# Window attention and a two-layer FFN on one core: in which order blocks and weight tiles are passed at the start

## The chip, the cores and the metric

The kernel runs on one core of a Trainium2 chip. The metric is the device time in microseconds. Three runs of the kernel before gave 1069.83, 1072.06 and 1072.11 us, so 1072.06 us is the median.

## The reference

Eight batches of 576 positions and eight heads of 64 go through causal attention with a window of 64 positions; the result, 4608 tokens by 512, goes through a matrix, a softplus and a second matrix.

```python
scores = scale * np.matmul(q, k.transpose(0, 1, 3, 2))
mask = (rel >= 0) & (rel < window)           # rel = query position - key position, window = 64
scores = np.where(mask, scores, -1000000000.0)
attn = np.exp(scores - np.max(scores, axis=-1, keepdims=True))
attn = attn / (np.sum(attn, axis=-1, keepdims=True) + 1e-09)
x = np.matmul(attn, v)                       # to 4608 x 512
h = x @ w_in                                 # 512 x 2048
g = np.maximum(h, 0.0) + np.log1p(np.exp(-np.abs(h)))
out = g @ w_out                              # 2048 x 512
```

All inputs and the output are float32 to the caller; the weights lie in DRAM as float64, and the kernel takes each weight apart into a high and a low part itself.

## The kernel before, in words

The 4608 tokens are cut into 12 blocks of 384 (`TB`). `g` numbers the blocks in the order in which they are worked on. For each block there is an attention part, made of four head pairs (`hp`, two heads each), and an FFN part, made of 16 steps, one for each tile of 128 hidden features (`f`, "weight tile" below). One step (`g`, `f`) is `ffn_up`, 12 matmuls of 384 columns into a bank `ps_h` (line 450; of `ps_h` there are two), a softplus on ScalarE and VectorE (lines 454 to 461; line 458 is the one that reads `ps_h` last), and `ffn_down`, 9 matmuls of 512 columns that add into three banks `ps_o` (line 471). The x of a block, which is what attention makes and `ffn_up` reads, stands in eight tiles, high and low for each head pair, and there are two such sets ("sides").

A weight tile has to be made before its first use: `load_w(f)` loads two pieces of float64, and each piece takes one instruction on ScalarE (161), four on VectorE (162 to 165; the first four pieces have line 162 on GpSimd), a rounding on ScalarE (166) and a subtraction on GpSimd (167). The two pieces come out as `osb` on VectorE. Weight tiles 8 to 15 stand in memory that the attention of blocks 0 and 1 uses before.

Attention of blocks 0 and 1 uses TensorE for its transposes (`by_pe`); from block 2 on q and k are transposed by DMA, whose input is `nat` and whose output is `tr` (line 314). In its stages a head pair runs scores (334), a masked minimum on VectorE (342), exp on ScalarE (345), sum, reciprocal and product (352, 353, 358), transposes back (379, 380), a split (385, 386), the product with v (427) and the x of this head pair (431, 432, 139, 140).

Since all weight tiles are not ready at the start, the FFN does not go through the blocks one by one. `passes` lists which block takes which range of tiles: block 0 over tiles 0 to 7, block 1 over all 16, block 0 over 8 to 15, and then block after block. A block whose range ends before tile 15 stores its partial sums to DRAM (`spill`), and they are added when the rest is done (`fill`). In this text step 0 to 191 are numbered in the order of `passes`.

What sets the order of the instructions is a list of events with due times: step n has its up part at 2n + 0.5 and its down part at 2n + 3.5; `load_w(f)` stands 12 before its first use; the head pairs of the first blocks begin at `BASE[g] + PACE[g] * hp`. The list is sorted and emitted. For events before 100 (steps up to 47) a scheduler then orders the instructions of every engine, so that an instruction can be put ahead of others that were emitted sooner; behind that TensorE keeps the emitted order. Each engine executes its own list strictly in that order on the chip.

Of the kernel before, what the change touches and what calls it, by code (L numbers as in the profile page):

```python
# [8 lines left out]
F32 = mybir.dt.float32  # L9
BF16 = mybir.dt.bfloat16  # L10
F32R = mybir.dt.float32r
# [4 lines left out]
P = 128  # L16
TB = 384
# [3 lines left out]

SPLIT = 8
AHEAD = 12
BASE = (-100, -46, 2 * (SPLIT + 16) - 24)
PACE = (5, 5, 4)
STG0 = (-8, 1, 3, 4, 5, 7, 8, 9, 10)
STG2 = (-8, 0, 2, 3, 4, 6, 7, 8, 9)
STG = (-13, -5, 0, 0, 3, 5, 7, 8, 11)
# [8 lines left out]
def window_attention_softplus_ffn(  # L37
# [16 lines left out]
    nc = tc.nc  # L54
    B, H, S, D = q.shape
    NT, DM = out.shape
    DF = w_in.shape[1]
    NP = H // 2
    NC = DM // P
    NF = DF // P  # L60
    NB = NT // TB
# [9 lines left out]
    xp = ctx.enter_context(tc.tile_pool(name="xp", bufs=1))  # L71
    ff = ctx.enter_context(tc.tile_pool(name="ff", bufs=2))
    late = ctx.enter_context(tc.tile_pool(name="late", bufs=1))
    dram = ctx.enter_context(tc.tile_pool(name="dram", bufs=1, space=bass.MemoryType.DRAM))
# [42 lines left out]
    def weight(m, i, f):  # L117

        if f < NE:
            return w_first[m][i][:, f, :]  # L120
        k = (f - NE) // 4
        if (m, i, k) not in w_last:
            w_last[m, i, k] = spare(4 * k + 2 * m + i, [P, 4, DM], F32R, f"w{m}{i}{k}")
        return w_last[m, i, k][:, f % 4, :]
# [19 lines left out]
    def raw_tiles(f):  # L144

        ks = (5,) if f < NE else [k for k in (5,) if k >= 4] if f < NE + 4 else []
        at = f % (len(ks) + 1)
        if at == len(ks):
            return [ff.tile([P, NC, P], w_in.dtype, name="raw", bufs=2) for _ in range(2)]
        t = spare(ks[at], [P, 2, NC, P], w_in.dtype, "raws")  # L150
        return [t[:, m, :, :] for m in range(2)]

    def float64_split(dst_hi, dst_lo, src, raw, n):


        nc.sync.dma_start(raw, src)
        words = raw.bitcast(U32).rearrange("p c (n two) -> p two c n", two=2)
        low, high = words[:, 0, :, :], words[:, 1, :, :]
        w = ff.tile([P, NC, P], F32, name="osb", bufs=2)
        wb = w.bitcast(U32)  # L160
        nc.scalar.activation(w, high.bitcast(F32), AF.Abs)
        (nc.gpsimd if n < 4 else nc.vector).tensor_scalar(w, w, ZERO_HIGH, None, ALU.max)  # L162
        nc.vector.tensor_scalar(wb, wb, 3, 0x3FFFFFF8, ALU.logical_shift_left, ALU.bitwise_and)  # L163
        nc.vector.scalar_tensor_tensor(wb, high, 0xC0000000, wb, ALU.bitwise_and, ALU.bitwise_or)  # L164
        nc.vector.scalar_tensor_tensor(wb, low, 29, wb, ALU.logical_shift_right, ALU.bitwise_or)  # L165
        nc.scalar.copy(dst_hi, w)
        nc.gpsimd.tensor_tensor(dst_lo, w, dst_hi.bitcast(F32), ALU.subtract)

    def load_w(f):
        fs = slice(f * P, (f + 1) * P)  # L170
        raws = raw_tiles(f)
        for m, src in enumerate((w_in[:, fs].rearrange("(c p) n -> p c n", p=P), w_out[fs, :].rearrange("p (c n) -> p c n", n=P))):
            hi, lo = [weight(m, i, f).rearrange("p (c n) -> p c n", n=P) for i in range(2)]
            float64_split(hi, lo, src, raws[m], 2 * f + m)
# [55 lines left out]
    xs = {}  # L230
    taken_ps = [0]

    def attention(g, hp):
# [39 lines left out]
        if by_pe:  # L273
# [17 lines left out]
            for hh in range(2):  # L291
                rows = slice(hh * D, (hh + 1) * D)
# [30 lines left out]
        for j in range(NJ):  # L323
            first = j == 0 and not prev
            c0 = WIN if first else 0
            n = W - c0
# [62 lines left out]

        if hp == 0:  # L390
            xs[g] = [[None] * NP, [None] * NP]
        side = 0 if g == 0 else 1 if g == 1 else (g + 1) % 2
        x_t = [xp.tile([P, TB], F32R, name=f"x{i}_{hp}_{side}") for i in range(2)]
        for i in range(2):
            xs[g][i][hp] = x_t[i]
        if by_pe:
# [3 lines left out]
        for hh in range(2):  # L400
# [6 lines left out]
            for kb in reversed(range(NJ)):  # L407
                n = W if kb < NJ - 1 else P
# [26 lines left out]
            yield  # L435


    gs = {}
    ops = {}
    part = {}  # L440
# [23 lines left out]
    def ffn_down(g, f, first, last):  # L464
        gt = gs.pop((g, f))
        if first:
            ops[g] = [ps_o.tile([P, DM], F32, name=f"ps_o{j}") for j in range(NJ)]
        for j in range(NJ):
            js = slice(j * P, (j + 1) * P)
            for i, (a, b) in enumerate(((0, 0), (0, 1), (1, 0))):  # L470
                mm(  # L471
                    ops[g][j], gt[a][:, js], weight(1, b, f),
                    start=(first and i == 0), stop=(last and i == 2),
                )
        if last:
            rows = out[ORDER[g] * TB : (ORDER[g] + 1) * TB, :]
            spill, fill = f < NF - 1, f == NF - 1 and g in part
            if spill:
                part[g] = rows = dram.tile([TB, DM], F32, name="part")
            for j0, j1 in ((0, 2), (2, 3)):  # L480
                o = ff.tile([P, NC, P], w_in.dtype, name="raw", bufs=2).bitcast(F32)
                o = o.rearrange("p c n -> p (c n)").rearrange("p (j n) -> p j n", n=DM)[:, : j1 - j0, :]
                rs = slice(j0 * P, j1 * P)
                if fill:
                    nc.sync.dma_start(o, part[g][rs, :].rearrange("(j p) n -> p j n", p=P))
                for j in range(j0, j1):
                    if fill:
                        nc.vector.tensor_tensor(o[:, j - j0, :], o[:, j - j0, :], ops[g][j], ALU.add)
                    else:
                        (nc.scalar.copy if j == 1 else nc.vector.tensor_copy)(o[:, j - j0, :], ops[g][j])  # L490
                nc.sync.dma_start(rows[rs, :].rearrange("(j p) n -> p j n", p=P), o)
# [2 lines left out]

    passes = [(0, 0, SPLIT), (1, 0, NF), (0, SPLIT, NF)] + [(g, 0, NF) for g in range(2, NB)]
    steps = [(g, f, f == f0, f == f1 - 1) for g, f0, f1 in passes for f in range(f0, f1)]


# [2 lines left out]
    events = []  # L503
    for g in range(NB):
        for hp in range(NP):
            if g < 3:
                base = BASE[g] + PACE[g] * hp
            else:
                base = 2 * NF * (g - 1) + SHP * hp + SH
            stages = attention(g, hp)  # L510
            for at in STG if g >= 3 else STG2 if g >= 2 else STG0:
                events.append((base + at, lambda stages=stages: next(stages, None)))
    loaded = 0
    for n, (g, f, first, last) in enumerate(steps):
        if f == loaded:
            events.append((2 * n - AHEAD, lambda f=f: load_w(f)))
            loaded += 1
        events.append((2 * n + 0.5, lambda g=g, f=f: ffn_up(g, f)))
        events.append((2 * n + 3.5, lambda step=steps[n]: ffn_down(*step)))
    events.sort(key=lambda e: e[0])  # L520
    for at, emit in events:
        if at < PE_ORDERED_FROM:
# [34 lines left out]
```

## Time and profile before

| | us |
|---|---|
| three runs, median (lowest, highest) | 1072.06 (1069.83, 1072.11) |
| the profiled execution's own time | 1069.74 |
| its span, first to last instruction | 1067.9 |
| TensorE (PE) busy | 1028.4, 96% of the span |
| VectorE (DVE) busy | 789.0, 74% |
| ScalarE (ACT) busy | 650.0, 61% |
| GpSimd (POOL) busy | 224.7, 21% |

The span is what the rows of the profile divide up; the profiled execution's own time is 1.84 us longer, and the median of the three runs lies 2.3 us above that. "Busy" adds up the time in which an engine had an instruction; a row of a group gives source line, engine, operation, output and input tiles, shape, count, busy time, mean duration in ns and the idle time ahead of it. Since instructions of an engine overlap a little, means times counts come out above the busy time.

### The profile page before, as it was taken

How to read it: one execution, taken by the hardware profiler on the slowest of the kernel's cores; microseconds unless marked ns; L12 is line 12 of the kernel's file. 1: busy time of each engine (PE TensorE's matmuls, PEld its weight loads, DVE VectorE, ACT ScalarE, POOL GpSimd, SP SyncE). 2: the span in 40 equal slices, each digit the busy share in tenths (PEclk: the TensorE clock that was granted, in tenths of full speed). 3: DMA queues.
4: the chain of work that ended last, by engine and by line, in shares of the span. 5: the costliest groups of instructions: out<-in, count | busy, mean ns of one | idle time of the engine just before them, and what ended most of it. 6: DMA issues, size and time to landing. Idle time of an engine off the chain costs nothing.

```text
span 1067.9 us, 18172 instructions
## 1 busy us (share of the span) xinstructions
PE 1028.4 (96%) x6096; PEld 924.3 (87%) x6096; DVE 789.0 (74%) x2319; ACT 650.0 (61%) x1669; POOL 224.7 (21%) x217
## 2 busy tenths in 40 slices
PE   7797988999999999999999999999999999999998
PEld 5576867888999899999999999999999999999996
DVE  4999899866777777777777777777777777865433
ACT  6786666666665666566656666656666665655333
POOL 4354355631111111112111111111211111110000
PEclk9999998999999999999999999999999999999999
DMA  7754645255334434343344334424434533520000
GB/s 197 198 140 105 169 105 146 67 127 119 70 71 101 96 79 105 64 97 81 81 96 96 84 76 93 107 60 88 102 74 84 115 80 62 131 51 1 30 1 30
DMA packets 296222, 98.20 MB, mean 92 GB/s; under 512 B 280512, under 2 KB 288704, under 8 KB 296128
## 3 DMA queue, kind: packets, MB, share of 16 engines
q1 hardware_dynamic: 296128, 97.03, 40.0%
q8 instruction: 48, 0.79, 0.3%
q14 instruction: 46, 0.38, 0.1%
HBM read 50.07 MB, written 10.22 MB: 56 GB/s over the span
## 4 chain that ended last, share of the span: by engine, by line
PE 78%; DVE 12%; DMA 4%; ACT 3%; issue 2%; SPq 1%; POOL 0%; DVEq 0%; ACTq 0%
PE ps_h L450 32%; PE ps_o L471 31%; PE ps_a L334 5%; PE ps_a L427 4%; PE ps_a L380 2%; DMA tr<-nat 2%; PE ps_a L379 2%; DVE p_t L358 2%; DVE osb L165 2%; DVE osb L164 1%; DVE osb L162 1%; DVE p_t L342 1%; DVE osb L163 1%; SPq L198 1%; DVE u L458 1%
## 5 line engine op out<-in xcount | busy, mean ns | idle before, releaser
L450 PE MATMUL ps_h<-x,w 128*128 128x384 f32 x2304 | 458.4, 344 | 15.4 <-DVE u L458 11.8
L471 PE MATMUL ps_o<-w,g 128*128 128x512 f32 x1728 | 438.7, 397 | 6.3 <-ACT g L460 4.3
L450 PEld LDWEIGHTS ps_h<-x,w 128*128 128x128 f32 x2304 | 400.6, 189 | 27.5 <-DVE u L458 12.5
L471 PEld LDWEIGHTS ps_o<-w,g 128*128 128x128 f32 x1728 | 318.1, 188 | 65.6 <-ACT g L460 4.6
L458 DVE SCALAR_TENSOR_TENSOR u<-ps_h,u 128x384 f32<-128x384 f32 x192 | 106.0, 552 | 139.7 <-ACT u L456 139.5
L454 ACT ACTIVATE u<-ps_h 128x384 f32<-128x384 f32 x192 | 93.6, 488 | 179.4 <-PE ps_h L450 177.2
L345 ACT ACTIVATE p_t<-p_t,mn 128x192 f32<-128x192 f32 (+1 forms) x288 | 127.0, 443 | 63.5 <-DVE mn L342 63.2
L140 POOL TENSOR_TENSOR x<-xf,x 128x384 fp32r<-128x384 f32 x40 | 41.1, 1027 | 460.6 <-DVE rs L352 362.9
L358 DVE TENSOR_SCALAR p_t<-p_t,rs 128x192 f32<-128x192 f32 (+1 forms) x288 | 110.4, 429 | 2.9
L342 DVE CUSTOM_DVE_ANT_0 p_t<-ps_a,mask 128x192 f32<-128x192 f32 (+1 forms) x244 | 77.3, 343 | 46.5 <-PE ps_a L334 36.1
L455 ACT ACTIVATE u<-u 128x384 f32<-128x384 f32 x192 | 100.7, 526 | 4.1
L456 ACT ACTIVATE u<-u 128x384 f32<-128x384 f32 x192 | 100.6, 524 | 3.2
L461 DVE TENSOR_TENSOR g<-u,g 128x384 fp32r<-128x384 f32 x160 | 89.5, 559 | 3.8 <-DVE g L460 0.5
L385 ACT CAST pt<-ps_a 128x512 fp32r<-128x512 f32 (+1 forms) x144 | 59.0, 417 | 33.7 <-PE ps_a L380 21.9
L312 POOL TENSOR_TENSOR nat<-q_in,nat 128x384 bf16<-128x384 f32 x40 | 38.6, 965 | 187.8 <-ACT nat L311 152.1
L386 DVE TENSOR_TENSOR pt<-ps_a,pt 128x512 fp32r<-128x512 f32 (+1 forms) x144 | 67.9, 477 | 12.3 <-ACT pt L385 10.7
L334 PE MATMUL ps_a<-tr 128*128 128x192 bf16 (+1 forms) x720 | 74.8, 246 | 0.9 <-DVE xf L432 0.7
L460 DVE CAST g<-u 128x384 fp32r<-128x384 f32 x176 | 67.9, 386 | 5.9
L380 PE MATMUL ps_a<-ident,p_t 128*128 128x128 f32 x276 | 66.6, 276 | 1.4 <-DVE p_t L358 1.3
L427 PEld LDWEIGHTS ps_a<-pt,vt 128*128 128x128 f32 (+1 forms) x608 | 64.0, 163 | 3.9 <-issue 0.5
L427 PE MATMUL ps_a<-pt,vt 128*128 128x64 f32 (+4 forms) x608 | 64.5, 247 | 0.4 <-DVE mn L342 0.4
L431 ACT COPY xf<-ps_a 64x384 f32<-64x384 f32 x80 | 38.1, 477 | 40.3 <-PE ps_a L427 37.5
(91 smaller groups left out, 1019.3 us busy)
## 6 DMA issues: line engine op xcount, KB each, us to landing
out_dram<-raw SPq DMA_DIRECT2D x12, 512.0 KB, 3.2
q_in<-in_q_dram SPq DMA_DIRECT2D x56, 96.0 KB, 2.6
raw<-in_moe_w_in_dram SPq DMA_DIRECT2D x10, 512.0 KB, 4.2
raw<-in_moe_w_out_dram SPq DMA_DIRECT2D x10, 512.0 KB, 4.2
k_in<-in_k_dram SPq DMA_DIRECT2D x32, 128.0 KB, 3.5
v_in<-in_v_dram SPq DMA_DIRECT2D x32, 128.0 KB, 2.8
raws<-in_moe_w_in_dram SPq DMA_DIRECT2D x6, 512.0 KB, 4.2
raws<-in_moe_w_out_dram SPq DMA_DIRECT2D x6, 512.0 KB, 5.0
```

What stands on the lines that cost most here:

```text
L334: mm(spv[:, hh, :], tr_q[a][:, hh, j * P : (j + 1) * P], tr_k[b][:, hh, kc], start=(hh == 0 and i == 0), stop=(hh == 1 and i == 2), skip_g ...
L342: nc.vector.tensor_tensor_reduce(pv, spv[:, hh, :], m[:, c0:], 1.0, 3.0e38, ALU.add, ALU.min, mn[:, j, hh : hh + 1])
L345: nc.scalar.activation(pv, pv, AF.Exp, bias=mn[:, j, hh : hh + 1], scale=-1.0, accum_out=sm[:, j, hh : hh + 1])
L358: nc.vector.tensor_scalar(pv, pv, rs[:, jj, hh : hh + 1], None, ALU.mult)
L427: mm(av[: D if lo else P, osl], vt[:, vb, hh, : 1 if lo else 2, :], pt[hh][lo][:, psl], start=(i == 0), stop=(i == len(order) - 1), skip_g ...
L450: mm(hv, weight(0, a, f)[:, c * P : (c + 1) * P], x[b][c], start=(i_mm == 0), stop=(i_mm == 3 * NC - 1))
L454: nc.scalar.activation(u, hv, AF.Abs)
L455: nc.scalar.activation(u, u, AF.Exp, scale=-1.0)
L456: nc.scalar.activation(u, u, AF.Ln, bias=1.0)
L458: nc.vector.scalar_tensor_tensor(gf, hv, 0.0, u, ALU.max, ALU.add)
L461: (nc.vector if g >= 2 else nc.gpsimd).tensor_tensor(gt[1], gf, gt[0].bitcast(F32), ALU.subtract)
L471: mm(ops[g][j], gt[a][:, js], weight(1, b, f), start=(first and i == 0), stop=(last and i == 2),)
```

## The change

The passes become: blocks 0 and 1 over tiles 0 to 7, block 2 over all 16, then block 1 over 8 to 15, then block 0 over 8 to 15, then block 3 and so on. With that:

- `BASE` and `PACE` get an entry for block 3, and block 2's attention is due from 8 on, where it was due from 24 on.
- `load_w` of tiles 8 to 15 is due at 10, 14.5, and so on to 41.5, where it was 12 ahead of its first use (20, 22, and so on to 34).
- The side of x is `g % 2`, so that block 2 takes the side of block 0, and block 3 that of block 1. Block 0's x is needed again later: `keep_x` stores its eight tiles (384 floats by 128 partitions each) to DRAM, and `fetch_x` loads them back after block 2's last step.
- Block 1 now has partial sums too; they get a DRAM tile of their own.

```diff
-BASE = (-100, -46, 2 * (SPLIT + 16) - 24)
-PACE = (5, 5, 4)
+LATE, LATE_PACE = 10, 4.5
+BASE = (-100, -46, 4 * SPLIT - 24, 69)
+PACE = (5, 5, 4, 5)
...
-        side = 0 if g == 0 else 1 if g == 1 else (g + 1) % 2
-        x_t = [xp.tile([P, TB], F32R, name=f"x{i}_{hp}_{side}") for i in range(2)]
+        x_t = [xp.tile([P, TB], F32R, name=f"x{i}_{hp}_{g % 2}") for i in range(2)]
...
+    x_kept = dram.tile([2 * NP, P, TB], F32, name="x_kept")
+
+    def keep_x():
+        for i in range(2):
+            for hp in range(NP):
+                nc.sync.dma_start(x_kept[i * NP + hp, :, :], xs[0][i][hp].bitcast(F32))
+
+    def fetch_x():
+        xs[0] = [[xp.tile([P, TB], F32R, name=f"x{i}_{hp}_0") for hp in range(NP)] for i in range(2)]
+        for i in range(2):
+            for hp in range(NP):
+                nc.sync.dma_start(xs[0][i][hp].bitcast(F32), x_kept[i * NP + hp, :, :])
...
-                part[g] = rows = dram.tile([TB, DM], F32, name="part")
+                part[g] = rows = dram.tile([TB, DM], F32, name=f"part{g}")
...
-    passes = [(0, 0, SPLIT), (1, 0, NF), (0, SPLIT, NF)] + [(g, 0, NF) for g in range(2, NB)]
+    passes = [(0, 0, SPLIT), (1, 0, SPLIT), (2, 0, NF), (1, SPLIT, NF), (0, SPLIT, NF)]
+    passes += [(g, 0, NF) for g in range(3, NB)]
...
-            if g < 3:
+            if g < len(BASE):
...
-            events.append((2 * n - AHEAD, lambda f=f: load_w(f)))
+            at = 2 * n - AHEAD if f < SPLIT else LATE + LATE_PACE * (f - SPLIT)
+            events.append((at, lambda f=f: load_w(f)))
...
+    events.append((SPLIT + 0.7, keep_x))
+    events.append((2 * (2 * SPLIT + NF) + 0.7, fetch_x))
```

How it moves the instructions is seen at three places. The lines of the changed kernel are one higher from line 27 on and 14 higher from the FFN on: its 163 to 166 are 162 to 165 of before, 343 is 342, 353 and 354 are 352 and 353, 359 is 358, 464 is 450, 472 is 458, 474 and 475 are 460 and 461, and 485 is 471.

First, VectorE around the line 458 of step 16 (the 17th step). Before, where step 16 is block 1 with tile 8, it is row 378 of VectorE's list:

```order
L432 TENSOR_TENSOR xf_1704<-ps_a_1787,xf_1704 64x384
L164 SCALAR_TENSOR_TENSOR osb_1548<-raw_1533,osb_1548 128x512
L386 TENSOR_TENSOR pt01_1811<-ps_a_1816,pt00_1810 128x64
L310 SCALAR_TENSOR_TENSOR q_in_1515<-q_in_1515,nat_1954 128x384
L313 COPY nat_1954<-nat_1954 128x6x64
L310 SCALAR_TENSOR_TENSOR k_in_1516<-k_in_1516,nat_1954 128x512
L313 COPY nat_1954<-nat_1954 128x8x64
L165 SCALAR_TENSOR_TENSOR osb_1548<-raw_1533,osb_1548 128x512
L458 SCALAR_TENSOR_TENSOR u_1778<-ps_h_1765,u_1778 128x384
L162 TENSOR_SCALAR osb_1627<-osb_1627 128x512
```

Now, where step 16 is block 2 with tile 0, it is row 508; the two rows with `raw_2238` belong to the last of the 32 weight pieces, and `rs_2751` and `pt01_2893` to the first head pair of block 3:

```order
L165 SCALAR_TENSOR_TENSOR osb_2249<-raw_2238,osb_2249 128x512
L353 TENSOR_SCALAR rs_2751<-sm_2750 128x2
L166 SCALAR_TENSOR_TENSOR osb_2249<-raw_2238,osb_2249 128x512
L387 TENSOR_TENSOR pt01_2893<-ps_a_2898,pt00_2892 128x64
L354 RECIPROCAL rs_2751<-rs_2751 128x2
L472 SCALAR_TENSOR_TENSOR u_2044<-ps_h_2031,u_2044 128x384
L359 TENSOR_SCALAR p_t00_101<-p_t00_101,rs_2751 128x192
L359 TENSOR_SCALAR p_t01_102<-p_t01_102,rs_2751 128x192
L472 SCALAR_TENSOR_TENSOR u_2103<-ps_h_2090,u_2103 128x384
L474 CAST g0_2049<-u_2044 128x384
```

What moved: 130 more rows stand ahead of step 16's line 458, among them the last six weight pieces and most of block 3's first head pair.

Second, TensorE at the up part of step 18. Before, its bank is `ps_h_1967`, its x that of block 1, and the transposes behind it are of block 2's attention:

```order
L450 MATMUL ps_h_1967<-x0_3_1_700,w000_1217 128x384
L450 MATMUL ps_h_1967<-x1_3_1_701,w000_1217 128x384
L450 MATMUL ps_h_1967<-x0_3_1_700,w010_1218 128x384
L380 MATMUL ps_a_1889<-ident_85,p_t11_104 128x128
L379 MATMUL ps_a_1889<-ident_85,p_t11_104 128x128
```

Now its bank is `ps_h_2124`, its x that of block 2, and the transposes behind it are of block 3's attention; `ps_h_2175` is step 19, and `g0_2049` with `ps_o0_2112` and its neighbours is the down part of step 16:

```order
L464 MATMUL ps_h_2124<-x0_3_0_1918,w00_109 128x384
L464 MATMUL ps_h_2124<-x1_3_0_1919,w00_109 128x384
L464 MATMUL ps_h_2124<-x0_3_0_1918,w01_110 128x384
L380 MATMUL ps_a_2899<-ident_85,p_t00_101 128x128
L381 MATMUL ps_a_2899<-ident_85,p_t00_101 128x128
L464 MATMUL ps_h_2175<-x0_0_0_1369,w00_109 128x384
L464 MATMUL ps_h_2175<-x1_0_0_1370,w00_109 128x384
L485 MATMUL ps_o0_2112<-w10_111,g0_2049 128x512
L485 MATMUL ps_o0_2112<-w11_112,g0_2049 128x512
```

What moved: all of block 2's attention is ahead of step 18 on TensorE, where it was partly behind; and as there are two banks `ps_h`, the up part of step 18 waits in both kernels for the line 458 of step 16.

Third, SP, the queue of all DMAs, at its start. Before:

```order
L224 DMA v_pad0_119<-in_v_dram 128x3x64
L204 DMA k_in_418<-in_k_dram 128x3x64 x2
L198 DMA v_in_1111<-in_v_dram 128x2x64
L224 DMA v_pad0_119<-in_v_dram 128x3x64 x2
L204 DMA qk_in_423<-in_q_dram 128x3x64 x2
```

Now:

```order
L225 DMA v_pad0_119<-in_v_dram 128x3x64
L205 DMA k_in_419<-in_k_dram 128x3x64 x2
L199 DMA v_in_831<-in_v_dram 128x2x64
L443 DMA x_kept_123<-x0_0_0_226 128x384
L443 DMA x_kept_123<-x1_0_0_227 128x384
L225 DMA v_pad0_119<-in_v_dram 128x3x64 x2
L205 DMA qk_in_424<-in_q_dram 128x3x64 x2
```

What moved: stores of block 0's x (line 443) stand between the loads, eight of them in the first 52 rows, and each waits there for its x tile.

## The prediction

> **What bounds the kernel now.** I read the page first: the two busiest engines over the whole span, then by slices.
>
> ```profile
> PE 1028.4 (96%) x6096; PEld 924.3 (87%) x6096; DVE 789.0 (74%) x2319; ACT 650.0 (61%) x1669; POOL 224.7 (21%) x217
> PE   7797988999999999999999999999999999999998
> DVE  4999899866777777777777777777777777865433
> PEclk9999998999999999999999999999999999999999
> ```
>
> TensorE is full from the ninth slice on, and VectorE is full just before, so there are two regimes with one boundary. The view by windows puts numbers on it (columns: window, its length, then busy us of PE, PEld, DVE, ACT, POOL, clock, DMA share, GB/s), and the view of waits says who holds TensorE up, first in 20 to 215 us, then from 215 us on.
>
> ```profile
> 20.00:215.00 195.00, 167.83 (x908) 140.66 (x907) 183.37 (x445) 134.19 (x341) 95.05 (x73) 0.96 0.53 136
> 215.00:1060.00 845.00, 844.33 (x5127) 773.08 (x5125) 595.53 (x1830) 503.87 (x1294) 121.29 (x123) 1.00 0.37 80
> PE ps_h L450 <- DVE u L458: 11.8, 8, 2.8
> PE ps_o L471 <- ACT g L460: 4.3, 1, 4.3
> PE ps_o L471 <- DVE g L460: 1.1, 2, 0.7
> ```
>
> Up to 215 us VectorE is busy for 183.4 of 195 us (94%), TensorE stands still for 27, and its largest wait is for line 458, the last reader of a `ps_h` bank. From 215 us on TensorE is busy for 844.3 of 845 us. So whatever changes the order of work within the first regime moves the end only by what it does to one moment: the time at which TensorE becomes free to run to the end, set against the TensorE work that is then still to do. Three rows of the timelines fix that moment before.
>
> ```profile
> 165.44 0.55 DVE L458 SCALAR_TENSOR_TENSOR u<-ps_h,u 128x384 f32<-128x384 f32 x1
> 213.07 0.55 DVE L458 SCALAR_TENSOR_TENSOR u<-ps_h,u 128x384 f32<-128x384 f32 x1
> 208.89 2.35 PE L450 MATMUL ps_h<-x,w 128*128 128x384 f32 x12 [0.74 <-DVE u L458]
> ```
>
> The first is step 16's line 458 (ends 165.99), the second step 25's (ends 213.62), the third the up part of step 25, after whose 0.74 us wait TensorE hardly stops: from 208.9 us it needs 1067.9 - 208.9 = 859.0 us to the end.
>
> **The change part by part.** No matmul and no weight piece is added or removed; the order is. VectorE executes its list strictly in order, and in the new list step 16's line 458 is row 508, behind all 32 weight pieces, all attention of block 2 and most of block 3's first head pair. TensorE cannot go past it: steps 16 and 17 hold both `ps_h` banks, and step 18 needs one of them. So the late due times of tiles 8 to 15 are not what the engine gets: the scheduler filled the row of VectorE with them ahead of step 16.
>
> *Term 1, when step 16's line 458 is done.* I count the rows ahead of it in the new list, compare with the rows ahead of an instruction of the old list whose time I know, and price the difference by the means of 20 to 215 us:
>
> ```profile
> L358 DVE TENSOR_SCALAR p_t<-p_t,rs 128x192 f32<-128x192 f32 x48 | 23.3, 533 | 0.2
> L163 DVE TENSOR_SCALAR osb<-osb 128x512 uint32<-128x512 uint32 x32 | 20.2, 631 | 0.9 <-POOL osb L162 0.7
> L162 DVE TENSOR_SCALAR osb<-osb 128x512 f32<-128x512 f32 x28 | 16.8, 599 | 5.3 <-ACT osb L161 5.3
> L164 DVE SCALAR_TENSOR_TENSOR osb<-raw,osb 128x512 uint32<-128x512 uint32 x20 | 15.8, 788 | 0.1
> L165 DVE SCALAR_TENSOR_TENSOR osb<-raw,osb 128x512 uint32<-128x512 uint32 x20 | 15.6, 781 | 0.0
> L458 DVE SCALAR_TENSOR_TENSOR u<-ps_h,u 128x384 f32<-128x384 f32 x26 | 14.2, 547 | 0.9 <-ACT u L456 0.9
> L342 DVE CUSTOM_DVE_ANT_0 p_t<-ps_a,mask 128x192 f32<-128x192 f32 x36 | 11.2, 347 | 0.0
> L460 DVE CAST g<-u 128x384 fp32r<-128x384 f32 x16 | 8.2, 513 | 0.2
> L352 DVE TENSOR_SCALAR rs<-sm 128x2 f32<-128x2 f32 x12 | 5.1, 429 | 0.5 <-ACT p_t L345 0.5
> L386 DVE TENSOR_TENSOR pt<-ps_a,pt 128x512 fp32r<-128x512 f32 x6 | 4.1, 679 | 0.0
> L310 DVE SCALAR_TENSOR_TENSOR k_in<-k_in,nat 128x512 f32<-128x512 f32 x5 | 3.4, 682 | 0.0
> L432 DVE TENSOR_TENSOR xf<-ps_a,xf 64x384 f32<-64x384 f32 x5 | 2.7, 544 | 1.6 <-ACT xf L431 1.5
> L140 DVE TENSOR_TENSOR vt<-v_in,vt 128x512 fp32r<-128x512 f32 x3 | 2.0, 678 | 0.0
> L490 DVE COPY raw<-ps_o 128x512 f32<-128x512 f32 x2 | 1.3, 678 | 0.0
> ```
>
> Against step 25 of the old list the new one has ahead of it 6 more of line 342 (6 x 0.347 = 2.1), 6 of 358 (3.2), 2 large of 386 (1.4), 3 of 432 (1.6), one more q and k of 310 (0.55 + 0.68 = 1.2), 2 of 140 (1.4), 2 of 490 (1.4) and 4 of 352 (1.7), together 14.0; the small ones beside them (accumulator reads, narrow 386, 313, 139, 353) add an estimated 4.0 by rows of the same view at 0.08 to 0.5 us each. It has 9 fewer of line 458 (4.9) and 8 fewer of 460 (4.1). 14.0 + 4.0 - 9.0 = 9.0, so 213.6 + 9.0 = 222.6 us. Against step 16 of the old list it has 6 more weight pieces (162 to 165: about 2.85 each, 17.1) and 40.3 of attention and drain rows: 166.0 + 57.4 = 223.4 us. Means times counts hide a little overlap, and idle time takes about as much: between the two old anchors the rows add up to 48.4 us and 47.6 passed. I take 223.0. The bounds: VectorE stands still for 11.6 us of the 195; if a third of that went, 4 us less; what could make it more is in the rivals.
>
> *Term 2, TensorE's work from step 18 on.* Before, 859.0 us remained at step 25. Now step 18 is next, so 7 more steps remain, while 36 matmuls of line 334, 16 transposes and 18 of line 427 that stood behind step 25 are done already.
>
> ```profile
> 1014.17 2.25 PE L450 MATMUL ps_h<-x,w 128*128 128x384 f32 x12
> 1018.31 2.25 PE L450 MATMUL ps_h<-x,w 128*128 128x384 f32 x12
> 234.35 0.92 PE L334 MATMUL ps_a<-tr 128*128 128x192 bf16 x9
> 207.22 0.93 PE L427 MATMUL ps_a<-pt,vt 128*128 128x64 f32 x8
> 239.60 0.27 PE L379 MATMUL ps_a<-ident,p_t 128*128 128x128 f32 x1
> 239.71 0.27 PE L380 MATMUL ps_a<-ident,p_t 128*128 128x128 f32 x1
> ```
>
> A bare step takes 1018.31 - 1014.17 = 4.14 us: 7 x 4.14 = 29.0. The others take at most 0.92 / 9 = 0.10, 0.11 and 0.93 / 8 = 0.12 us each: 36 x 0.10 + 16 x 0.11 + 18 x 0.12 = 7.5, and 0.5 less since the last of a row reaches past the next start: 7.0. The sum is 859.0 + 29.0 - 7.0 = 881.0 us.
>
> *Term 3, the start of the run.* From step 16's line 458 to step 18's VectorE has 11.6 us of rows (6 of 358, 4 of 342, 4 of 458 and 460, 2 of 310 and of 352 from the means above, and two of the split of g, which block 2 has on VectorE where blocks 0 and 1 have it on GpSimd). TensorE has two steps and four transposes until it needs that bank, 2 x 4.14 + 0.4 = 8.7. It waits 2.9 us. After that a step costs VectorE about 1.6 us of FFN rows against 4.14 on TensorE, so VectorE falls behind no more.
>
> *Parts at nothing.* The stores of `keep_x` and the loads of `fetch_x` (16 transfers of 192 KB) stand on SP, which mostly waits for free buffers; the loads have eight steps, 33 us, until block 0 needs them. Uncovered, the stores would hold back early loads by 0 to 4 us and add that to term 1. The second spill and fill adds two rows of line 490 on VectorE, counted above. The two more changes of pass (steps 32 and 40) can cost TensorE between nothing and the 4.3 us of its longest wait above; I take nothing, since step 32 before showed none.
>
> **The sum** is 223.0 + 2.9 + 881.0 = 1106.9 us of span against 1067.9, 39.0 us more. The profiled execution took 1069.7 and the median run 1072.1, so 1108.7 to 1111.1; I forecast 1110 us.
>
> The clock of TensorE is worth a look, since it will stand still longer:
>
> ```profile
> 95.75 3.40 PE L471 MATMUL ps_o<-w,g 128*128 128x512 f32 x9 [4.28 <-ACT g L460]
> 138.79 1.84 PE L450 MATMUL ps_h<-x,w 128*128 128x384 f32 x9 [2.83 <-DVE u L458]
> ```
>
> After 4.28 us of waiting nine matmuls took 3.40 us, after 2.83 us there is no such thing. The Trainium skill ("TensorE: Matmul & The Clock Gate", section "What's actually happening") has a rule that speaks against the change: after an idle window of about 3.4 us the clock halves until TensorE has been busy for such a window. These two rows agree. By the rule the sum would be up to 1.7 us more, if the window before step 18 is idle; the attention matmuls of block 3 that stand there are a reason against it.
>
> **The rivals.** *The stretch is deeper.* The last six weight pieces share two raw buffers with the partial sums of block 1, which now leave in that stretch.
>
> ```profile
> DVE osb L162 <- ACT osb L161: 5.3, 5, 2.1
> 116.68 3.96 DMA part<-raw
> ```
>
> Each reuse is a store of 4.0 us, a load and the ScalarE row before VectorE's next, and block 2's head pairs are a chain through one `tr`. VectorE's wait for this was 5.3 us in 195; two or three full rounds uncovered would add 8 to 15 us: 1118 to 1125. For it: the pieces stand right behind each other there. Against it: attention rows stand between most.
>
> *VectorE gets faster.* Line 358 takes 533 ns here and less where GpSimd is nearly idle (500 to 700 us):
>
> ```profile
> L358 DVE TENSOR_SCALAR p_t<-p_t,rs 128x192 f32<-128x192 f32 x52 | 20.1, 427 | 0.7
> L460 DVE CAST g<-u 128x384 fp32r<-128x384 f32 x39 | 14.3, 366 | 1.2
> L352 DVE TENSOR_SCALAR rs<-sm 128x2 f32<-128x2 f32 x29 | 4.7, 161 | 0.0
> ```
>
> Ahead of the row 508 nine of GpSimd's splits of g fewer stand than ahead of step 25 before, out of 95 us of its work, so about a tenth of the overlap goes: 1 to 2 us. If all went, 60 of line 358 would save 0.106 us each, 15 of line 352 0.268 and 8 of line 460 0.147: 11.6 us, 1098. The Trainium skill ("SBUF — State Buffer", section "Who interferes with whom") states that such VectorE instructions and GpSimd hold one port pair in turn, each for its whole instruction; the longer rows agree with it.
>
> *The new order covers the idle time*, which is the other side: TensorE's 27 us of standstill between 20 and 215 us vanish, since block 2's 16 steps need none of the late tiles, and the time is 1072 - 27 = 1045. Its place is step 16, and the point from which it decides is a line 458 there at 223 - 39 = 184 us or sooner. Against it: 57 us of rows more than before stand ahead, and only 18 would be allowed.
>
> **How the numbers follow.** The forecast has 0.70, the deeper stretch 0.16, faster VectorE 0.10, covered idle time 0.03; 0.01 is left for no effect at all. Faster VectorE at 1098 (a little less with term 1's lower bound) and the deeper stretch at 1125 bound the range: 1096 to 1126. About 0.2% is what a measurement of this kernel can tell from no change; every case but the last two is beyond it: slower 0.96, within 0.2% 0.01, faster 0.03.
>
> **What would show it.** Step 16's line 458 (472 in the new numbering) ends at 219 to 228 us; TensorE's standstill from 20 us to there grows from 27 us to about 65; from there on TensorE is full to the end, 881 us later; waits of the matmuls of `ps_h` for x and for line 472 between 160 and 223 us. The forecast is wrong if that row comes before 215 us, if TensorE stops again for more than 5 us behind it (steps 32, 40 and 48, or SP's loads of x), or if the remainder is not 881 us.

## The result, and the profile after

The changed kernel takes 1097.76 us (median of 4 runs, 1096.60 to 1098.22), the kernel before 1070.94 us on the same chip (4 runs, 1069.12 to 1072.11): a ratio of 1.025, 95% interval 1.0231 to 1.027. It is slower, as forecast, but by 27 us and not by the 38 of the forecast (39 in the span). The profiled execution took 1096.6 us, with a span of 1094.4 us against 1067.9. It is the fastest of the four, whose spans go from 1094.4 to 1096.1 us, so a difference of one or two us between the spans of two profiled executions shows nothing by itself; where it matters, the medians stand beside it.

First the page of the changed kernel: busy time by engine, and the rows of the slices that were shown of before.

```profile
PE 1040.4 (95%) x6096; PEld 933.0 (85%) x6096; DVE 794.8 (73%) x2322; ACT 650.8 (59%) x1669; POOL 218.3 (20%) x217
PE   6897887699999999999999999999999999999998
DVE  5999999955545777877877867877777877776433
PEclk9998988799999999999999999999999999999999
```

The two regimes are there again, with the boundary in the same slice. What differs lies ahead of it. The view by windows (window, length, busy us of PE, PEld, DVE, ACT, POOL, granted clock, DMA share, GB/s):

```profile
20.00:215.00 195.00, 153.55 (x799) 125.42 (x800) 191.85 (x481) 132.96 (x347) 84.24 (x69) 0.89 0.64 160
215.00:1060.00 845.00, 844.20 (x5094) 772.85 (x5094) 583.81 (x1778) 495.45 (x1269) 125.80 (x128) 1.00 0.36 79
```

VectorE is busy for 191.85 of 195 us, where it was 183.37. TensorE stands still for 41.5 us, where it was 27.2. Behind 215 us TensorE is full, as before. Now the moment itself, in six rows of the timelines (start, duration, engine, line, count; in brackets the wait ahead of the row and what ended it):

```profile
203.70 0.35 DVE L140 CAST x<-xf 128x384 fp32r<-128x384 f32 x1
204.10 2.74 PE L464 MATMUL ps_h<-x,w 128*128 128x384 f32 x6 [1.50 <-DVE x L140]
209.58 0.93 ACT L470 ACTIVATE u<-u 128x384 f32<-128x384 f32 x2
210.57 0.53 DVE L472 SCALAR_TENSOR_TENSOR u<-ps_h,u 128x384 f32<-128x384 f32 x1
210.65 2.08 PE L335 MATMUL ps_a<-tr 128*128 128x192 bf16 x12 [0.37 <-DMA tr<-nat]
212.44 2.91 PE L464 MATMUL ps_h<-x,w 128*128 128x384 f32 x12
```

Line 140 makes the last x that block 2 still lacks. The six matmuls behind it are the last quarter of the up parts of steps 16 and 17, which stand interleaved: the other three quarters were done by 192.6 us. ScalarE's last rows of the softplus for these two steps (line 470) end at 210.1 and 210.5 us, step 16's line 472 ends at 211.1, and step 18's up part starts at 212.4. No wait stands ahead of it: TensorE was busy until then with twelve score matmuls of block 3 (line 335), which come first in its list and had waited for the landing of their transposed operand `tr`. So step 18 did not wait for its bank, which was free 1.3 us sooner. In the chain of the profile (start, duration, what) line 472 does not occur; it runs through that load, which left at 206.1 us behind other loads on the queue (line 205), and these behind a row of VectorE (line 343) that ended at 204.6 us:

```profile
204.32 0.27 DVE p_t L343
204.61 0.86 SPq L205
205.53 0.50 SPq L205
206.08 4.53 DMA tr<-nat
210.65 2.08 PE ps_a L335 x12
```

From step 18's start 1094.4 - 212.4 = 882.0 us pass to the end.

### The profile page after: what moved, and what is told of

It reads as the page before. It is cut to its first block, busy times and chain, and to the rows that moved or that the text cites. A ratio compares the mean times of both kernels' runs of the same rounds, so it can differ in the third digit from the quotient of the medians.

```text
span 1094.4 us, 18223 instructions
## 1 busy us (share of the span) xinstructions
PE 1040.4 (95%) x6096; PEld 933.0 (85%) x6096; DVE 794.8 (73%) x2322; ACT 650.8 (59%) x1669; POOL 218.3 (20%) x217
## 4 chain that ended last, share of the span: by engine, by line
PE 77%; DVE 13%; DMA 3%; ACT 2%; issue 2%; SPq 2%; POOL 0%; DVEq 0%; ACTq 0%; POOLq 0%
PE ps_o L485 32%; PE ps_h L464 32%; PE ps_a L335 5%; PE ps_a L427 4%; DVE osb L165 2%; PE ps_a L381 2%; PE ps_a L380 2%; DVE p_t L359 2%; DMA tr<-nat 2%; DVE p_t L343 1%; SPq L205 1%; DVE osb L166 1%; DVE osb L163 1%; DVE osb L164 1%; DVE u L472 1%
## 5 line engine op out<-in xcount | busy, mean ns | idle before, releaser
L468 ACT ACTIVATE u<-ps_h 128x384 f32<-128x384 f32 x192 | 93.6, 489 | 212.2 <-PE ps_h L464 209.4
L359 DVE TENSOR_SCALAR p_t<-p_t,rs 128x192 f32<-128x192 f32 (+1 forms) x288 | 107.3, 418 | 2.7
L427 PE MATMUL ps_a<-pt,vt 128*128 128x64 f32 (+4 forms) x608 | 67.5, 252 | 4.2 <-DVE pt L387 4.2
L380 PE MATMUL ps_a<-ident,p_t 128*128 128x128 f32 x248 | 62.3, 281 | 9.0 <-DVE p_t L359 6.9
L381 PE MATMUL ps_a<-ident,p_t 128*128 128x128 f32 x276 | 67.8, 279 | 2.0 <-DVE p_t L359 0.8
```

Of the source, the lines that this page charges most:

```text
L359: nc.vector.tensor_scalar(pv, pv, rs[:, jj, hh : hh + 1], None, ALU.mult)
L381: tp(pp[:, j * W : j * W + P], p_t[hh][:, j, P:], ident)
L427: mm(av[: D if lo else P, osl], vt[:, vb, hh, : 1 if lo else 2, :], pt[hh][lo][:, psl], start=(i == 0), stop=(i == len(order) - 1), skip_g ...
L468: nc.scalar.activation(u, hv, AF.Abs)
```

## The experiments

All were timed in three rounds beside the kernel before, whose median lay between 1070.8 and 1071.3 us. The table has, for those with the new order of passes that moved something, what the sections below compare: the span, VectorE's busy time in 20 to 215 us, the time at which TensorE goes on with block 2's last x, the end of step 16's line 472, the start of step 18's up part, and what is left from there.

| kernel | ratio to before | span | VectorE busy | last x | line 472 | step 18 up | rest |
|---|---|---|---|---|---|---|---|
| changed | 1.025 | 1094.4 | 191.9 | 204.1 | 211.1 | 212.4 | 882.0 |
| e1 late due times undone | 1.0125 | 1081.3 | 177.1 | 181.5 | 189.0 | 189.8 | 891.5 |
| e2 no keep_x, fetch_x | 1.0216 | 1093.2 | 189.9 | 199.7 | 207.9 | 209.3 | 883.9 |
| e3 line 163 on GpSimd | 1.0234 | 1095.0 | 185.7 | 202.8 | 210.4 | 211.4 | 883.6 |
| e5 no late line 163 | 1.0225 | 1093.3 | 186.5 | 194.7 | 208.6 | 208.7 | 884.6 |
| e8 late tiles between | 1.0162 | 1087.4 | 183.7 | 193.9 | 199.5 | 199.6 | 887.8 |
| e9 no spill | 1.026 | 1096.0 | 190.4 | 204.7 | 210.6 | 212.6 | 883.4 |
| e10 neither | 1.0219 | 1092.8 | 185.8 | 201.0 | 205.5 | 209.4 | 883.4 |
| e11 written order | 1.0341 | 1106.6 | 186.1 | 202.3 | 208.5 | 213.2 | 893.4 |
| e12 e1 and written order | 1.0252 | 1097.2 | 169.6 | 182.4 | 190.2 | 195.6 | 901.6 |

**Which part costs what: the late tiles' due times undone (e1).**

```diff
-            at = 2 * n - AHEAD if f < SPLIT else LATE + LATE_PACE * (f - SPLIT)
+            at = 2 * n - AHEAD
```

> One part undone: load_w of tiles 8 to 15 stands 12 ahead of its first use again; all else as in the changed kernel. In VectorE's list 19 weight pieces stand ahead of step 16's line 458 where the changed kernel has 32. Theory R (VectorE's rows ahead of that line set its moment): 13 pieces of about 2.35 us (2.77 by the means of the changed kernel's rows, less the 15% by which its rows overlap) are 31 us, so the line is done at 211 - 31 = 180 us; the pieces come back in steps 16 to 28, where VectorE has about 2.5 us to spare in each step of 4.14, so TensorE waits some 15 us there; span 1075 to 1082, 12 to 20 us below the changed kernel. Theory C (the chain of block 2's attention through DMA, TensorE and ScalarE sets the moment, the weight rows only fill it): the line at 203 us or later, span 1088 or more.

1083.71 us, ratio 1.0125 (1.0103 to 1.0147). About half of the loss, 13.1 us of span, is due to the pieces ahead of step 16; the other 13.4 us stay with the rest of the change (the order of passes, the new due times of the attention and the transfers of x). The line came at 189.0 us, between both expectations. 35 us of VectorE's time went from ahead of it (its busy time up to the line fell from 195.3 to 160.4 us), and the line moved by 22: VectorE's idle time up to there grew from 15.7 to 28.7 us. In the view of waits VectorE now stands for block 2's attention (columns: waiting row, what it waited for, us, times, longest):

```profile
DVE q_in L311 <- ACT nat L310: 7.9, 3, 2.8
DVE p_t L343 <- PE ps_a L335: 1.8, 2, 1.1
```

So rows do set most of the moment, but taking them away uncovers 13 us of waits that they had covered, of which the waits for block 2's attention are the largest that the view shows.

**The transfers (e2).** In this kernel block 0's second part reads block 2's x.

```diff
-                nc.sync.dma_start(x_kept[i * NP + hp, :, :], xs[0][i][hp].bitcast(F32))
+                pass
...
-        xs[0] = [[xp.tile([P, TB], F32R, name=f"x{i}_{hp}_0") for hp in range(NP)] for i in range(2)]
-        for i in range(2):
-            for hp in range(NP):
-                nc.sync.dma_start(xs[0][i][hp].bitcast(F32), x_kept[i * NP + hp, :, :])
+        xs[0] = xs[2]
```

> The 16 transfers of block 0's x are left out (keep_x and fetch_x); block 0's second half reads block 2's x instead, so the output of block 0 is not the reference's. Theory R: 30 pieces in place of 32 stand ahead of step 16's line 458, about 2 us less, span 1090 to 1094. Theory S (the stores in SP's queue hold the early loads back, and that is part of what the change costs): step 0's to step 7's lines 458 come 2 to 4 us sooner, span 1086 to 1090 or less.

1094.00 us, ratio 1.0216 (1.0198 to 1.0233). The span is 1.2 us shorter, and the medians lie 3.8 us apart (1097.76 and 1094.00). So the eight stores and eight loads cost some 1 to 4 us, within the 0 to 4 of the prediction, and the larger price that S expected (a span of 1086 to 1090 or less) is out.

**Work moved to GpSimd (e3, e4).**

```diff
-        (nc.gpsimd if n < 4 else nc.vector).tensor_scalar(w, w, ZERO_HIGH, None, ALU.max)
+        (nc.gpsimd if n < 4 or n >= 2 * SPLIT else nc.vector).tensor_scalar(w, w, ZERO_HIGH, None, ALU.max)
```

> One size changed: line 163 (the max on w) of the 16 late weight pieces is on GpSimd, as it is for the first four pieces. VectorE has 16 rows of 0.53 us less, about 15 of them ahead of step 16's line 458 (31 pieces ahead, row 493). Theory R: that line 8 to 9 us sooner, at 203 us, span 1086 (1083 to 1089); if GpSimd's rows lengthen VectorE's others, 1 to 3 us of it is lost. Theory C: the line stays at 208 or later, span 1091 or more.

1096.44 us, ratio 1.0234 (1.0211 to 1.0257): the span of 1095.0 us is no shorter, and R's 203 us for the line became 210.4, as C had it. Part of what VectorE was spared came back in its other rows. Here is the group of line 359 in 20 to 215 us, in the changed kernel and then in e3 (count, busy us, mean ns, idle),

```profile
L359 DVE TENSOR_SCALAR p_t<-p_t,rs 128x192 f32<-128x192 f32 x54 | 21.5, 446 | 0.0
```
```profile
L359 DVE TENSOR_SCALAR p_t<-p_t,rs 128x192 f32<-128x192 f32 x54 | 27.6, 559 | 0.1
```

and the windows row of e3:

```profile
20.00:215.00 195.00, 156.27 (x805) 129.16 (x804) 185.73 (x465) 133.50 (x347) 112.84 (x84) 0.87 0.64 160
```

The same 54 rows took 6.1 us more, while GpSimd was busy for 112.84 us instead of 84.24. VectorE's busy time still fell by 6.1 us, to 185.73, and these became idle time: the line stayed.

The other move is of a row behind the release, the split of g of block 2:

```diff
-        (nc.vector if g >= 2 else nc.gpsimd).tensor_tensor(gt[1], gf, gt[0].bitcast(F32), ALU.subtract)
+        (nc.vector if g >= 3 else nc.gpsimd).tensor_tensor(gt[1], gf, gt[0].bitcast(F32), ALU.subtract)
```

> One part alone: the split of g (line 475) of block 2 is on GpSimd, as for blocks 0 and 1, so VectorE has 16 rows of 0.57 us less, all of them behind step 16's line 458, and TensorE's list is nearly unchanged. Theory R with its third term at nothing (no wait of TensorE behind step 18): span 1093 to 1095, same as the changed kernel within 0.2%. If the third term of the prediction were right in part: up to 2.9 us less, 1091 to 1092.

1096.02 us, ratio 1.0235 (1.0216 to 1.0254), span 1095.6, line 472 at 210.9: no effect that can be told from none. Nothing behind the release waits for VectorE's FFN rows.

**Rows taken away, with nothing in their place (e5).**

```diff
-        (nc.gpsimd if n < 4 else nc.vector).tensor_scalar(w, w, ZERO_HIGH, None, ALU.max)
+        if n < 2 * SPLIT:
+            (nc.gpsimd if n < 4 else nc.vector).tensor_scalar(w, w, ZERO_HIGH, None, ALU.max)
```

> The changed kernel without line 163 (the maximum with the smallest high word) for the 16 late weight pieces; that part of the conversion is left out, nothing takes its place on another engine. It takes 16 rows of 0.53 us, 8.5 us, out of VectorE's list ahead of step 16's line 472 (the remap of rows gives 7.6 net). R (rows): VectorE was busy for 98% of 20 to 215 us, so the line comes at 202 to 205 us instead of 211.1, the remainder stays 882, the span is 1085 to 1088. C (chain): the loads, the ScalarE rows and block 2's attention chain set the moment; waits take the place of the rows, the line comes at 207.5 us or later, the span is 1090 or more.

1095.65 us, ratio 1.0225 (1.021 to 1.024). The span of 1093.3 us is 1.1 us shorter (the medians lie 2.1 apart). The expectation of C came true; it had named loads, but not the buffers that they wait for. Block 2's last x came 9.4 us sooner, as rows would have it, but line 472 only 2.5. Three rows of the timelines of e5 show why:

```profile
189.81 0.66 ACT L162 ACTIVATE osb<-raw 128x512 f32<-128x512 f32 x1 [1.97 <-DMA raw<-in_moe_w_in_dram]
190.50 0.43 DVE L165 TENSOR_SCALAR osb<-osb 128x512 uint32<-128x512 uint32 x1 [1.83 <-ACT osb L162]
208.70 4.19 PE L465 MATMUL ps_h<-x,w 128*128 128x384 f32 x12 [2.58 <-DVE u L473]
```

The last four pieces share two raw buffers with block 1's partial sums, which step 15 gives at 181 us. Their load lands at 189.8 us, so their rows come behind block 2's x and ahead of line 472 (473 there). This is the prediction's "deeper stretch" mechanism; here it takes the place of the rows that went.

**The raw buffers set free (e9), and both (e10).** In both, block 1's first sum is left out.

```diff
+            if spill and g == 1:
+                return
             if spill:
```

> The changed kernel without block 1's spill: its sum over the first 8 weight tiles is neither copied nor stored nor added later (left out), so the two raw buffers go straight from one weight piece to the next. In the changed kernel the last four late pieces wait for these buffers (their load starts at 185.1 us, behind step 15's partial sums). By itself this should do little, since VectorE stood still for 0.7 us in 160 to 215 us: only two rows of 0.7 us go. Rows (R) and raw buffers (L) both expect the line of step 16 at 208.5 to 210.5 us, a span of 1091 to 1093.5. If the buffers alone set the moment, the line comes at 205 us or sooner.

> Both left out: the 16 late rows of line 163 and block 1's spill. Two limits side by side (RL: rows, and behind them the raw buffers that the last four pieces share with step 15's partial sums): each alone moved the line by 2.5 us or less, both together by 8 to 10 us: the line at 201 to 203.5 us, the span at 1083 to 1086. If a third limit stands right behind (A: block 2's and block 3's attention chain through one tr), the line comes at 206 us or later and the span is 1088 or more.

e9: 1098.47 us, ratio 1.026 (1.0243 to 1.0277), no gain, where both theories had expected a small one (a span of 1091 to 1093.5). By e5 and e9 together, the buffers are hidden behind the rows in the changed kernel. e10: 1094.76 us, ratio 1.0219 (1.0204 to 1.0235). With both gone the line came at 205.5 us, 5.6 sooner, less than the 8 to 10 of RL and half a microsecond sooner than A's bound of 206. Only 1.6 us of span were gained (3.0 between the medians), as A expected. What took the rest stands ahead of step 18 in e10:

```profile
207.59 2.08 PE L336 MATMUL ps_a<-tr 128*128 128x192 bf16 x12 [3.00 <-DMA tr<-nat]
209.37 4.00 PE L465 MATMUL ps_h<-x,w 128*128 128x384 f32 x12
```

TensorE's next work in its list was the scores of block 3's next head pair (line 336 there), whose transposed load landed at 207.5 us. That is a third limit: step 18 starts 3.9 us behind the line. The same load stands ahead of step 18 in the changed kernel (0.37 us of waiting, above) and, with waits of 0.54, 1.03 and 1.70 us, in e2, e4 and e9. Only in e5 and e8 does step 18 start right behind line 472.

**Block 3 kept out of the stretch (e11, e12).** One constant; e12 has e1's edit as well.

```diff
-PE_ORDERED_FROM = 100
+PE_ORDERED_FROM = 34
```

> The changed kernel with the written order followed from place 34 on instead of 100 (one constant): the scheduler can no longer pull block 3's first head pair forward. By the lists it removes from ahead of step 16's line 472 on VectorE 8 rows of line 343, 4 of 359 and their small ones (5.2 us of rows as priced, 196.0 to 191.2), and on TensorE the matmuls of line 335 on block 3's tr ahead of step 18's up part, which waited for the transposed load until 210.65 us. All of block 2's rows and all 32 pieces stay ahead. A (the release is block 2's last x, then whatever stands between it and line 472, then block 3's tr ahead of step 18): block 2's last x stays at 202 to 204 us, the line comes at 206.5 to 208.5, step 18's up part right behind it, the remainder is 882 to 885 (its matmuls of block 3 come later), the span is 1088 to 1092. If only the total of VectorE's rows counts: the line at 206, the span at 1088. If block 3 has no part in it: 1094.

> The same constant, with the late tiles' due times undone as well, so that the pass order is all that is left of the change. The run with the due times undone alone took 1081.3 us of span: step 16's line 472 at 189.0 us, and 9.5 us of waits and half clock behind it, where the late pieces, block 2's end and block 3's first pairs stood together. With block 3 behind, VectorE's rows by step 26 drop from 226 to 206 us as priced. If these rows cost the 9.5 us: a span of 1070 to 1075, within 0.7% of the kernel before. If block 2's chain alone sets the moment and the late tiles the rest, 1079 to 1082. Slower than that if the written order makes block 3's attention late at step 48.

e11: 1107.94 us, ratio 1.0341 (1.0325 to 1.0356). e12: 1098.84 us, ratio 1.0252 (1.0235 to 1.0269), 15 us above e1; its span of 1097.2 us is above both ranges that were expected (1070 to 1075 and 1079 to 1082). In e11 block 2's last x and the line came as A had them, but step 18's up part did not follow, and the rest grew; no theory had that. Four rows of TensorE's timeline in e11, and its row of the windows for 300 to 360 us:

```profile
202.31 1.01 PE L464 MATMUL ps_h<-x,w 128*128 128x384 f32 x2 [5.08 <-DVE x L140]
209.13 4.29 PE L485 MATMUL ps_o<-w,g 128*128 128x512 f32 x9 [3.71 <-DVE g L474]
213.22 3.03 PE L464 MATMUL ps_h<-x,w 128*128 128x384 f32 x12
297.41 1.15 PE L335 MATMUL ps_a<-tr 128*128 128x192 bf16 x12 [1.34 <-DMA tr<-nat]
```
```profile
300.00:360.00 60.00, 53.64 (x338) 48.28 (x338) 45.94 (x138) 39.34 (x107) 22.91 (x20) 0.97 0.49 110
```

Step 16's down part now stands ahead of step 18's up part, so the gain on the line is lost at once; and block 3's attention, not pulled forward, costs 6.4 us of standstill in 300 to 360 us, where the changed kernel has none, and its own time. So keeping block 3's rows out of the stall gains nothing in this form. Whether they cost anything where they stand is not shown: the constant also fixes the order of the FFN parts, which these two runs don't separate.

**Between (e8).**

```diff
-LATE, LATE_PACE = 10, 4.5
+LATE, LATE_PACE = 20, 3.5
```

> The changed kernel with the late weight tiles due from 20 in steps of 3.5 instead of from 10 in steps of 4.5: half of them stand ahead of step 16, between the changed kernel (all) and the run that undid the late due times (none). By the two measured points (priced rows 196.0 us: line at 211.1; 165.0 us: 189.0) and the priced rows here, 180.2 us, R expects the line at 199 to 201 us. The rest of the pieces then stands ahead of steps 18 to 24, so that TensorE stops there for some us; the span is 1080 to 1085. C: with the pieces no longer spread, waits for their loads come in, the line at 204 or later, span 1086 or more.

1088.84 us, ratio 1.0162 (1.0147 to 1.0177), line 472 at 199.5 us, inside what was read off the two measured points; the span, 1087.4 us, is 2 us above R's range and in C's (1086 or more), since the rest behind step 18 grew from 882.0 to 887.8.

**The kernel before (e6, e7).**

> The kernel before, without its line 163 for the same 16 late pieces (left out). If VectorE's rows set the moment there too (R), step 25's line 458 comes about 8 us sooner, at 204 to 207 us, and the time is 1062 to 1065 us. If waits do (C; VectorE had 24.1 us of idle time by step 25), half or more of the rows comes back as idle time, and the time is 1066 us or more.

> The kernel before, with block 1's first half of the split of g (line 460, 16 rows of 0.51 us, 8.2 us) on ScalarE, as block 0 has it, instead of VectorE; nothing is left out. ScalarE was busy for 134 of 195 us there. R: VectorE's list is 8 us shorter by step 24, and nothing on GpSimd's port grows, so 1062 to 1066 us. C: ScalarE's queue (exp and ln of the next steps and of the attention, weight pieces) hands the time back, TensorE's waits for line 460 grow from 5.4 us to 10 or more, and the time is 1069 us or more.

e6 has e5's edit. It took 1072.70 us (10 runs), ratio 1.0012 (1.0002 to 1.0022): 16 rows fewer on VectorE, and no gain. e7 moves block 1's casts to ScalarE:

```diff
-        (nc.scalar.copy if g == 0 else nc.vector.tensor_copy)(gt[0], gf)
+        (nc.scalar.copy if g <= 1 else nc.vector.tensor_copy)(gt[0], gf)
```

It took 1069.92 us (10 runs), ratio 0.9985 (0.9975 to 0.9996): at most a gain of 0.25%, about what can be told from none. In 20 to 215 us VectorE stayed as busy as it was (182.69 us against 183.37). Both meet C's expected time, e6 with the wait for line 458 (459 there) grown from 11.8 to 16.6 us:

```profile
PE ps_h L451 <- DVE u L459: 16.6, 6, 5.0
```

In e7 the wait for the casts did not grow, as C had it, so the reason C gave is not the one that held. Why the time stays was not settled for these two: the scheduler writes another order for each edit, so no such run removes rows alone.

## Why the prediction was right in sign and 12 us off

**Term 1 was mis-sized: 211.1 us, not 223.0, outside its own bound of 4 us**, and by the prediction's own sign (wrong "if that row comes before 215 us") this part failed. The place and the row were right: the line is row 508 of VectorE's list, and the end of the stall follows it by 1.3 us. The step that failed reads "means times counts hide a little overlap, and idle time takes about as much". It held between two points of the old list and did not carry over. Against step 25 of before, which is the anchor used, VectorE was busy 5.6 us longer (195.35 against 189.77 us, overlaps taken off) and not the 9.0 that the rows were priced at, and idle 8.1 us less (15.75 against 23.85) and not the same: 213.6 + 5.6 - 8.1 = 211.1. So most of the miss is idle time. The largest part of it that the views name is VectorE's wait for ScalarE's first row of a weight piece, 5.3 us before (line 162) and 0.6 us now (line 163). The late pieces can be done whenever a load has landed, and in the new list they stand between rows of block 2's attention; that each fills waits of the other is a reading and not shown row by row, but the runs show the other side: as pieces leave the stretch, VectorE's idle time in these 195 us goes from 3.2 us (changed) to 11.3 (e8) and 17.9 (e1).

The smaller part is shorter rows. Line 359 took 446 ns against the 533 it was priced at, line 163 528 against 599; line 165 went the other way. In 20 to 215 us, of the changed kernel:

```profile
L163 DVE TENSOR_SCALAR osb<-osb 128x512 f32<-128x512 f32 x28 | 14.8, 528 | 0.6 <-ACT osb L162 0.6
L165 DVE SCALAR_TENSOR_TENSOR osb<-raw,osb 128x512 uint32<-128x512 uint32 x20 | 18.3, 914 | 0.2
```

All durations up to the line add up to 230.4 us, against 234.2 at the means of before. GpSimd was busy for 84.24 us instead of 95.05, and with 112.84 (e3) the mean of line 359 was 559 ns. The rule of the Trainium skill that the prediction cited ("SBUF — State Buffer", section "Who interferes with whom") agrees with these three. It is not the whole of it: in e5, with 87.7 us of GpSimd, the mean was 509 ns.

**What term 1 counted is also not quite what sets the moment.** The prediction had TensorE held by the bank alone. Step 16 needs block 2's last x, then its matmuls and ScalarE's softplus. In the changed kernel and eight of the nine runs of the table line 472 ends 4.5 to 8.2 us behind that x, whatever else was changed; only e5 has 13.9. In e9, e10, e11 and e12 VectorE even stands still for 0.45 to 1.11 us just ahead of the line, waiting for ScalarE's line 470; in the changed kernel that row was done at most half a microsecond before the line began. The rows ahead of that x set it for the most part, and the prediction's count by row 508 includes these 7 us, so the count worked as a stand-in. Beside it stand block 3's load, which ends last in the changed kernel and more clearly in e10, the loads into the raw buffers (in e5) and the waits of the attention (in e1). In the changed kernel the softplus (210.1 and 210.5 us), the line (211.1) and the scores ahead of step 18 (212.4) are done within 2.3 us of each other. That fits with what the runs show: no single removal of rows gained what the rows took.

**Term 2 held**: 882.0 us against 881.0, without a stop at steps 32, 40 or 48. e11 agrees with it in direction only: with block 3's attention behind step 18 the rest is 893.4 us, but TensorE stands still for 8.3 us of 215 to 1060 us there, so the size of the deduction of 7.0 us is not tested.

**Term 3 was nothing instead of 2.9 us.** TensorE starts step 18 1.3 us behind the line, because of block 3's scores, and does not stop. From step 16's line 472 to step 18's 9.9 us passed, not 11.6, and e4 shows that those rows were no limit.

**The standstill** up to the release was to grow from 27 to about 65 us; it grew to 41. The line came 12 us sooner, and the same matmuls took 12 us longer (TensorE busy 1040.4 us against 1028.4), so that the two give 65 - 12 - 12. The slower matmuls are the clock:

```profile
184.00:190.80 6.80, 4.00 (x16) 2.73 (x16) 6.39 (x21) 3.00 (x9) 2.30 (x2) 0.50 0.92 201
190.80:204.40 13.60, 7.69 (x44) 6.63 (x44) 13.43 (x31) 7.92 (x18) 5.32 (x5) 0.75 0.81 203
204.40:211.20 6.80, 4.29 (x14) 2.56 (x14) 6.80 (x24) 5.90 (x19) 2.12 (x3) 0.50 0.98 158
215.00:260.00 45.00, 45.00 (x257) 40.54 (x257) 29.07 (x82) 22.54 (x59) 3.79 (x4) 1.00 0.23 47
```

Most of it fell into time that TensorE would have waited. The six matmuls at 204.1 us took 2.74 us (about 1.1 at the pace of twelve in 2.25), but VectorE worked without a pause up to line 472, so no delay of the line by them shows. On the path are block 3's twelve scores (2.08 us, where twelve of this kind took 1.15 us in e11 at 297.41 us) and step 18's twelve (2.91 against 2.25): an estimate of 0.9 + 0.7 = 1.6 us. The 1.7 that the prediction allowed for is close to it.

**The parts at nothing** held: `keep_x` and `fetch_x` are worth 1.2 us between the profiled spans and 3.8 between the medians (e2), inside the 0 to 4 given; from 215 us on TensorE stands still for 0.8 of 845 us, so the changes of pass cost nothing.

**The rivals.** The covered idle time fell by its own point: 211 us is far from 184. The deeper stretch did not come by itself (e9), but its buffers are the next limit once rows go (e5). "VectorE gets faster", at 1098, has the time that was measured but only 3 to 4 us of its mechanism; the 1097.76 is no proof of it. That the time lies in the range of 1096 to 1126 at all is luck in part, since this rival set the lower bound and the idle time did the rest.

**What stays open**: why the rest of the change still costs 13.4 us of span in e1. Ahead of the line at 189.0 us there stand the waits for the attention, at a granted clock of 0.67 from 180 to 190 us, and the rest behind step 18 is 9.5 us longer (3.7 of them waits for line 472); no run took the attention chain itself away. No run took block 3's load from ahead of step 18 without changing more, either. Nothing tried beats the kernel before by more than can be measured.

## What to carry to other kernels

A count of rows on an engine that executes in order gives the right place and a useful upper size, but idle time is no constant that cancels: work that can run at any time fills the waits of a chain, and moving it in or out moves the idle time too. Before a stall is priced by one engine, ask what the released instruction itself needs, and what the second and third limits are: here three were done within 2.3 us, so that taking 8 us of rows from the first gained 1 to 2. And a scheduler that writes the order anew answers each edit with another order; its pulled-forward rows look like a cost in the stall, and the run that kept them back, with the FFN parts in another order too, was 12 us slower.

## What the runs showed of the hardware

TensorE's clock fell to half without a long standstill. It went from 1.00 to 0.50 at about 182.9 us, when TensorE had been busy for 1.83 of the last 3.40 us, in pieces. Between 160 us and there no wait was longer than 1.63 us. The windows on either side of that moment, and that longest wait:

```profile
179.50:182.90 3.40, 1.83 (x19) 1.53 (x18) 3.40 (x12) 1.79 (x6) 0.00 (x0) 1.00 0.82 238
182.90:186.30 3.40, 2.00 (x13) 1.59 (x11) 3.40 (x10) 2.88 (x11) 1.29 (x1) 0.50 0.56 121
173.75 1.66 PE L485 MATMUL ps_o<-w,g 128*128 128x512 f32 x6 [1.63 <-DVE g L474]
```

The Trainium skill ("TensorE: Matmul & The Clock Gate", section "What's actually happening") says that the gate goes by how busy the array has been recently, and gives an idle window of about 3.4 us for the half clock. Read as a share of a window, the trace agrees with it; read as one uninterrupted pause, as the prediction did, it does not. Sparse work was enough here. What share is too little is not shown: from 169.3 to 172.7 us TensorE was busy for 1.77 of 3.40 us, and the clock stayed at 1.00.

VectorE's rows overlap by more than "a little": up to step 16's line the durations add up to 230.4 us, while it was busy for 195.3. A sum of durations overstates the busy time of such a stretch by 15% of the sum.
